# Lightning attention and a highway layer on one core: a second written-out order of all engines

## The chip, the core and the metric

The kernel runs on one core of a Trainium2 chip. The core has five engines that work side by side, each through its own queue of instructions in program order: TensorE (PE) for products, VectorE (DVE), ScalarE (ACT), GpSimd (POOL) and SyncE (SP), which here issues the transfers. They wait for each other by semaphores only. The metric is the device time of one execution in microseconds.

## The reference

Attention with a decay per head, over 4 batches, 8 heads, 768 positions of 64 elements, is followed by a highway layer over the 3072 tokens of 512 features that come out of it:

```python
for b in range(nb):
    intra = (qb @ kb.T * Dmask) @ vb                   # inside a block
    inter = (qb * lam_pow) @ kv_state                  # from all blocks before
    out[block] = intra + inter
    kv_state = lam_block * kv_state + (kb * rev_pow).T @ vb
x = out.transpose(0, 2, 1, 3).reshape(B * S, H * D)
H = maximum(x @ w_h, 0)
T = 1 / (1 + exp(-(x @ w_t + b_t)))
result = T * H + (1 - T) * x                           # = x + T * (H - x)
```

Everything is given and returned as 32-bit floats.

## The kernel before

The tokens are cut into 12 tiles (n = 0 to 11) of 256 positions, three to a batch; a tile has two rows b of 128. The order of the work is not found by a scheduler: it is written out in a string `PLAN`, and the loop at the end of the kernel emits one piece of work for each token of it. Each engine gets its pieces in the order in which they stand there, so PLAN is five queues in one. After the dots stand the tile (or group) and its parts, after `@` the engine, after `=` the numbers of the buffers or PSUM banks that the piece takes.

Loads, all on SP: `Lk.n.p`, `Lq.n.p`, `Lv.n.p` bring half (four heads, 256 KB) of a tile of k, q, v; `W.w.g` brings half (512 KB) of w_h (w = 0) or w_t (w = 1); `ST.n` stores a tile (512 KB), `ST.11.b.p` a part of the last one.

Preparing, mostly on POOL: `CK` casts k to bf16, `CQ` and `CV` cast q and v and scale them by powers of the decay (part 2 means the whole tile), `WC.w.g.i` casts a quarter of a weight. `LB` makes the powers: a product spreads the eight decay factors (the row `lam_r`) over the partitions, then come a logarithm and two exponentials. `PT` loads ACT's table for the sigmoid; `B` and `BC` turn the bias into a column.

Attention: `TK`, `TQ` transpose k and q on PE, `EK`, `EQ` copy the results out of PSUM. `SA.n` and `SB.n` compute a tile's scores together with its state products (the state stays in PSUM; `SA` needs the tile's scaled v), `KE.n.b` copies the state out, `M.n.e.u` applies the decay mask (always DVE), `I` multiplies by the state, `A.n.u` the masked scores by v, and `D.n.b` takes a finished row out as `xT`.

Highway: rows are joined into ten groups g (two rows in groups 0 to 3 and 7, four in 4 to 6, one in 8 and 9). `F.g.u.w` is a product with w_h or w_t, `H` makes max(h, 0) - x (DVE), `G` the sigmoid (ACT), `X` multiplies the two (DVE or POOL), `R` adds x and turns the result back on PE, `E` copies it out for the store.

`Z.r` issues r idle products of zeros in which nothing is computed; they fill time in which PE would wait.

Of the kernel before, what the change touches and what calls it, by code (L numbers as in the profile page):

```python
# [26 lines left out]
A.0.1=1 M.1.0.0=5 M.1.1.0=6 Z.3=0 TK.2.2=0 CK.3.2@POOL=0 KE.1.0@ACT=2 SB.1=5 EK.2.2@ACT=2 KE.1.1@ACT=3 M.1.0.1=7
WC.1.0.0@ACT A.0.0 D.0.0@ACT=0 I.1.0=2 I.1.1=4 WC.1.0.1@DVE A.1.0 A.1.1 Z.1=0 TQ.2.2=0 D.1.1@ACT=1 D.1.0@ACT D.0.1@DVE
Z.1=5 F.0.0.1=5 BC G.0.0 EQ.2.2@DVE I.2.0=3 CQ.3.2@POOL=1 WC.0.0.1@DVE F.0.0.0=6 H.0.0=0 X.0.0@DVE=0 WC.1.1.1@ACT
WC.1.1.0@ACT F.1.0.1=1 G.1.0 F.1.0.0=0 SA.2=426 H.1.0=1 CV.3.2@POOL=3 M.2.1.0=0 M.2.1.1=3 M.2.0.0=1 Lk.7.1 SB.2=5  # L30
F.1.1.1=0 F.0.1.1=2 WC.0.1.0@ACT KE.2.0@ACT=0 I.2.1=6 G.0.1 F.0.1.0=4 Lv.7.0=2 Lv.7.1 A.2.0 M.2.0.1=2 X.1.0@DVE=1
A.2.1 D.2.0@ACT=2 TK.3.2=5 F.1.1.0=1 Lq.8.0=3 CQ.4.2@POOL=0 D.2.1@DVE F.2.0.0=6 Lq.8.1 Lk.8.0=3 Lk.8.1 Lv.8.1=3 G.1.1
H.0.1=2 X.0.1@DVE H.1.1=0 EK.3.2@ACT=0 X.1.1@DVE TQ.3.2=3 EQ.3.2@ACT H.2.0=1 F.2.1.0=4 H.2.1=2 R.1=25 E.1.0@ACT=0
R.0=10 E.0.1@ACT=1 SA.3=364 KE.3.0@ACT=1 M.3.1.0=5 F.2.0.1=2 M.3.0.0=6 TQ.4.2=0 SB.3=6 M.3.1.1=4 CK.4.2@ACT=1 Lv.8.0
M.3.0.1=7 CV.4.2@POOL=0 TK.4.2=3 I.3.1=4 E.0.0@ACT A.3.0=1 EQ.4.2@ACT=1 KE.3.1@ACT=2 E.1.1@DVE EK.4.2@DVE A.3.1
D.3.1@DVE=1 F.2.1.1=6 SA.4=053 M.4.0.0=0 M.4.1.0=1 D.3.0@ACT CQ.5.2@POOL=2 F.3.0.1=1 G.2.1 X.2.1@DVE=1 F.3.0.0=4
H.3.0=0 KE.4.0@ACT=3 CK.5.2@POOL=2 Lk.9.1=4 Lk.9.0 G.2.0 Lq.9.1=4 X.2.0@DVE G.3.0 M.4.1.1=2 SB.4=0 KE.4.1@ACT=0
TK.5.2=5 EK.5.2@ACT=2 TQ.5.2=6 F.3.1.0=4 X.3.0@DVE=0 H.3.1=2 F.3.1.1=2 EQ.5.2@ACT M.4.0.1=3 CV.5.2@POOL=1 SB.5=3
# [43 lines left out]
def kernel(  # L82
# [11 lines left out]
    nc = tc.nc  # L94
    B, H, S, D = q.shape
# [9 lines left out]
    singles = ctx.enter_context(tc.tile_pool(name="singles", bufs=1))  # L105
# [3 lines left out]
    V, A, P, T = nc.vector, nc.scalar, nc.gpsimd, nc.tensor  # L109
# [279 lines left out]

    def powers():  # L390
        t = bank(("lam",), [128, H])
        T.matmul(t, lhsT=ones, rhs=lam_r, start=True, stop=True)
        A.activation(ln_bc, t, AF.Ln)
        V.tensor_tensor(p_ln, in0=ln_bc[:, None, :, None].to_broadcast([128, NST, H, J]),
                        in1=tk_f[:, :, None, :].to_broadcast([128, NST, H, J]), op=ALU.mult)
        A.activation(pow_q, p_ln, AF.Exp)
        A.activation(pow_v, p_ln, AF.Exp, scale=-1.0)
        A.dma_start(out=bt_r, in_=moe_b_t.rearrange("(j p) -> j p", p=128))

    def spin(r, idle=[0]):  # L400
        idle[0] += 1
# [57 lines left out]
```

## Time and profile before

| | us |
|---|---|
| three runs | 107.06, 107.11, 108.89; median 107.11 |
| the profiled execution | 106.9 |
| its span, first to last instruction | 105.1 |
| PE busy, of the span | 97.1 |
| DVE, ACT, POOL busy | 80.1, 70.3, 59.9 |
| mean rate of all transfers | 262 GB/s |

The span is one execution as the hardware profiler saw it, and the times of pieces below come from it. PE's busy time includes its idle products, and the ends of products are modelled, so a full PE says only that nothing keeps it waiting. In the views, a time in brackets is how long the engine was idle before an instruction, and the name after the arrow is what ended the wait; "issue" means that the profile shows nothing that it waited for.

### The profile page before, as it was taken

The page shows a single profiled execution, that of the slowest core. Times are in us where ns is not written, and L with a number is a line of the kernel's source. Part 1 is how long each engine was busy: PE and PEld are TensorE (multiplying, and loading weights), DVE is VectorE, ACT ScalarE, POOL GpSimd, SP SyncE. Part 2 cuts the span into 40 slices and gives each one's busy share as a digit, 9 for nine tenths or more (in the row PEclk, how much of TensorE's full clock was granted, in tenths as well). Part 3 has the DMA queues.
Part 4 walks back from the last instruction along what each step waited for, and adds up shares of the span by engine and source line. Part 5 has one row for each costly group of instructions (what it writes and reads, how often), then busy time and mean ns, then how long its engine had stood idle before and what let it go on. Part 6 is the DMA issues. An engine that isn't in the chain of part 4 may idle for free.

```text
span 105.1 us, 4749 instructions
## 1 busy us (share of the span) xinstructions
PE 97.1 (92%) x2087; PEld 69.1 (66%) x2087; DVE 80.1 (76%) x138; ACT 70.3 (67%) x120; POOL 59.9 (57%) x51
## 2 busy tenths in 40 slices
PE   4997999999999999999999999999899999995950
PEld 1434565778888887988465776575586567785930
DVE  4347187946979898997899799889697797995660
ACT  4228334787668998969579897366886556575860
POOL 6200886536479569859959789989496300700000
PEclk9999999999999999999999999999999999999996
DMA  1999999999999999999999999999960005994593
GB/s 40 287 316 291 290 290 329 324 334 314 291 292 292 298 288 278 293 280 295 263 305 301 296 267 279 317 315 331 363 204 14 0 6 190 377 377 171 204 359 130
DMA packets 43582, 27.57 MB, mean 262 GB/s; under 512 B 1446, under 2 KB 40618, under 8 KB 43562
## 3 DMA queue, kind: packets, MB, share of 16 engines
q1 hardware_dynamic: 43552, 27.27, 90.4%
q8 instruction: 16, 0.26, 1.1%
q14 instruction: 4, 0.03, 0.1%
q10 hardware_dynamic: 10, 0.00, 0.0%
HBM read 20.97 MB, written 6.29 MB: 259 GB/s over the span
## 4 chain that ended last, share of the span: by engine, by line
PE 84%; DMA 4%; ACT 3%; issue 2%; SPq 1%; DVE 1%; ACTq 0%; DVEq 0%
PE bt L332 21%; PE bh L332 20%; PE bs L238 7%; PE bo L306 7%; PE bktr L218 6%; PE bx L376 5%; PE bspin L404 5%; PE bqtr L218 5%; PE bo L295 5%; DMA kf<-in_k_dram 4%; PE kv L243 4%; SPq L183 1%; ACT L419 1%; ACT bt L343 1%; DVE th L346 1%
## 5 line engine op out<-in xcount | busy, mean ns | idle before, releaser
L332 PEld LDWEIGHTS <-w_b 128*128 128x128 bf16 x320 | 27.3, 98 | 12.5 <-issue 1.2
L280 DVE TENSOR_TENSOR m<-bs,tri 128x512 bf16<-128x512 f32 x48 | 30.6, 680 | 2.5 <-PE bs L238 1.9
L201 POOL TENSOR_TENSOR vs<-vf,pow_v 128x1024 bf16<-128x1024 f32 (+1 forms) x13 | 22.1, 1706 | 14.1 <-DMA vf<-in_v_dram 13.1
L332 PE MATMUL bt<-xT,w_b 128*128 128x256 bf16 (+2 forms) x160 | 24.5, 294 | 1.2 <-issue 1.1
L332 PE MATMUL bh<-xT,w_b 128*128 128x256 bf16 (+2 forms) x160 | 24.3, 294 | 0.0
L336 DVE SCALAR_TENSOR_TENSOR hm<-bh,xT 128x512 bf16<-128x512 f32 (+1 forms) x26 | 16.5, 645 | 6.5 <-PE bh L332 4.5
L201 POOL TENSOR_TENSOR qb<-qf,pow_q 128x1024 bf16<-128x1024 f32 (+1 forms) x11 | 20.1, 1827 | 2.1 <-DMA qf<-in_q_dram 2.1
L343 ACT ACTIVATE bt<-bt,bt_col 128x256 f32<-128x256 f32 (+2 forms) x34 | 15.4, 461 | 6.5 <-PE bt L332 3.8
L117 ACT ACTIVATE ss<-kv 128x512 bf16<-128x512 f32 x20 | 11.9, 596 | 4.8 <-PE kv L243 4.7
L346 DVE TENSOR_TENSOR th<-bt,hm 128x512 bf16<-128x512 f32 (+1 forms) x20 | 12.5, 632 | 1.2 <-ACT bt L343 0.2
L404 PE MATMUL bspin<-blank 128*128 128x512 bf16 x36 | 11.8, 464 | 1.4 <-DVE blank L130 1.4
L117 ACT ACTIVATE xT<-bo 128x512 bf16<-128x512 f32 x15 | 10.5, 748 | 2.8 <-PE bo L306 2.7
L238 PE MATMUL bs<-kq 64*64 64x128 bf16 x384 | 12.1, 219 | 0.0
L117 ACT ACTIVATE kq<-bktr 128x1024 bf16<-128x1024 bf16 (+1 forms) x9 | 8.4, 929 | 4.5 <-PE bktr L218 4.5
L346 POOL TENSOR_TENSOR th<-tb,hm 128x512 bf16<-128x512 f32 x6 | 6.9, 1159 | 7.6 <-DVE hm L336 7.3
L119 POOL CAST kb<-kf 128x1024 bf16<-128x1024 f32 (+1 forms) x9 | 8.5, 944 | 3.9 <-DMA kf<-in_k_dram 3.8
L238 PEld LDWEIGHTS <-kq 64*64 64x64 bf16 x384 | 9.0, 107 | 1.0 <-issue 0.2
L119 DVE CAST xT<-bo 128x512 bf16<-128x512 f32 x9 | 6.5, 732 | 3.3 <-PE bo L306 3.3
L243 PE MATMUL kv<-vs,kb 64*64 64x64 bf16 x320 | 8.7, 195 | 0.0
L117 ACT ACTIVATE o<-bx 128x512 f32<-128x512 f32 x13 | 7.4, 597 | 2.0 <-DMA out_dram<-o 1.0
L218 PE MATMUL bktr<-id,kb 128*128 128x128 bf16 x96 | 7.7, 220 | 0.8 <-ACT kb L117 0.7
L243 PEld LDWEIGHTS <-kb 64*64 64x64 bf16 x320 | 6.8, 109 | 2.6 <-issue 1.5
(55 smaller groups left out, 121.5 us busy)
## 6 DMA issues: line engine op xcount, KB each, us to landing
kf<-in_k_dram SPq DMA_DIRECT2D x24, 256.0 KB, 5.6
qf<-in_q_dram SPq DMA_DIRECT2D x24, 256.0 KB, 5.3
vf<-in_v_dram SPq DMA_DIRECT2D x24, 256.0 KB, 5.5
out_dram<-o SPq DMA_DIRECT2D x11, 512.0 KB, 4.2
w_f<-in_moe_w_t_dram SPq DMA_DIRECT2D x2, 512.0 KB, 7.4
w_f<-in_moe_w_h_dram SPq DMA_DIRECT2D x2, 512.0 KB, 7.7
out_dram<-oq SPq DMA_DIRECT2D x1, 256.0 KB, 2.2
out_dram<-oh SPq DMA_DIRECT2D x2, 128.0 KB, 1.8
```

The source lines that it names most:

```text
L117: A.activation(dst, src, AF.Copy)
L119: ENG[eng].tensor_copy(dst, src)
L201: ENG[eng].tensor_tensor(dst, in0=get(src, n)[:, heads(p)].rearrange("p h (j d) -> p h j d", j=J), in1=pw[:, n % NST, heads(p), :, None].t ...
L218: T.transpose(t[:, i, j, :], get(x + "b", n)[:, j, h:h + 2, :], id128)
L238: T.matmul(get("s", n, e, hp // 2)[half(b), hp % 2, j, :], lhsT=kq(n)[half(e), 0, hp, j, half(b)], rhs=kq(n)[half(e), 1, hp, :, half(b)], ...
L243: T.matmul(kv[half(e), hp, half(e)], lhsT=get("kb", n)[half(b), j, 2 * hp + e, :], rhs=get("vs", n)[half(b), 2 * hp + e, j, :], start=firs ...
L280: V.tensor_tensor(new(("m", n, e, u), [128, 2, J, C]), in0=get("s", n, e, u), in1=tri[:, None].to_broadcast([128, 2, J, C]), op=ALU.mult)
L332: T.matmul(t[:, r, :], lhsT=w_b[w][:, kc, m * 128:(m + 1) * 128], rhs=xT(g)[:, kc, :], start=(kc == 0), stop=(kc == KC - 1))
L336: V.scalar_tensor_tensor(new(("hm", g, u), [128, len(rows(g, u)), size(g) * C], tag=f"hm{size(g)}"), in0=get("h", g, u), scalar=0.0, in1=x ...
L343: A.activation(get("tt", g, u)[:, r, :], t[:, r, :], AF.Sigmoid, bias=bt_col[:, m:m + 1])
L346: ENG[eng].tensor_tensor(new(("th", g), [128, NP, size(g) * C], tag=f"th{size(g)}")[:, span(g, u), :], in0=get("tt", g, u), in1=get("hm", ...
L404: T.matmul(t, lhsT=blank[:, 0:128], rhs=blank, start=True, stop=True)
```

## The change

The whole of PLAN is replaced. The same pieces are there, with these differences: six `KE` move from ACT to DVE, other copies and casts change engines (three `EK` and two `D` go to ACT, two `E` to DVE, two weight casts to POOL), and 35 idle products stand in place of 36. The order on every engine, the order of the loads and the buffers are new; the order was planned with five sets of fetch delays. Beside it, the bias is brought by a transfer that ACT issues right behind that of the decay factors, not behind the exponentials; `PT` stands later; and the first three idle products and the product that spreads the factors read constants that the program sets up in any case, so that the tile `ones` goes.

The plan's opening, the place around the last tiles and the end, before and after:

```diff
-Z.4=0 LB=6 Z.8=0
-Lk.1.1=0 Lq.1.1=0 CQ.1.1@DVE=0 Lq.0.1=1 CQ.0.1@DVE=1 TQ.0.1=0 Lk.0.0=1 Lq.0.0 PT CK.0.0@ACT=0 CK.1.1@POOL=1
-Lv.0.0=0 Lk.0.1 Lv.0.1 CV.0.1@POOL=0 Lk.1.0 CK.1.0@POOL CQ.0.0@DVE Lq.1.0 CQ.1.0@POOL Lv.1.1=1 CV.1.1@POOL=1 Lv.1.0
-CV.1.0@POOL Lk.2.0=2 Lk.2.1 CK.2.2@POOL=2 Lq.2.0=2 Lq.2.1 CQ.2.2@POOL=2 W.1.0 W.0.0 Lv.2.1=2 WC.0.0.0@POOL Lv.2.0
-TQ.1.1=1 W.1.1 TK.1.1=2 CV.0.0@DVE W.0.1 Lk.3.0=3 Lk.3.1 Lq.3.1=3 Lq.3.0 Lv.3.0=3 Lv.3.1 Lq.4.1=4 Lq.4.0 TK.0.0=3
-CV.2.2@POOL=2 Lk.4.1=4 Lk.4.0 Lv.4.0=4 Lv.4.1 Lq.5.1=1 Lq.5.0 Lk.5.1=0 Lk.5.0 Lv.5.0=0 CK.0.1@ACT Lv.5.1 Z.9=4
-TK.0.1=4 Lq.6.1=0 Lk.6.0=1 TQ.0.0=5 Lk.6.1 WC.0.1.1@POOL B=6 Lq.6.0 EQ.0.1@ACT=0 EK.1.1@DVE=1 EK.0.0@DVE EK.0.1@ACT
-EQ.0.0@DVE Z.2=0 SA.0=230 KE.0.0@ACT=0 Lv.6.1=1 Lv.6.0 M.0.1.1=0 M.0.1.0=1 M.0.0.0=2 Z.5=4 TQ.1.0=4 EQ.1.0@DVE
-TK.1.0=5 SB.0=0 EQ.1.1@DVE I.0.1=3 EK.1.0@ACT M.0.0.1=3 KE.0.1@ACT=1 Z.3=2 SA.1=245 M.1.1.1=4 Lq.7.1=2 Lq.7.0 Lk.7.0=2
-A.0.1=1 M.1.0.0=5 M.1.1.0=6 Z.3=0 TK.2.2=0 CK.3.2@POOL=0 KE.1.0@ACT=2 SB.1=5 EK.2.2@ACT=2 KE.1.1@ACT=3 M.1.0.1=7
-WC.1.0.0@ACT A.0.0 D.0.0@ACT=0 I.1.0=2 I.1.1=4 WC.1.0.1@DVE A.1.0 A.1.1 Z.1=0 TQ.2.2=0 D.1.1@ACT=1 D.1.0@ACT D.0.1@DVE
-Z.1=5 F.0.0.1=5 BC G.0.0 EQ.2.2@DVE I.2.0=3 CQ.3.2@POOL=1 WC.0.0.1@DVE F.0.0.0=6 H.0.0=0 X.0.0@DVE=0 WC.1.1.1@ACT
-WC.1.1.0@ACT F.1.0.1=1 G.1.0 F.1.0.0=0 SA.2=426 H.1.0=1 CV.3.2@POOL=3 M.2.1.0=0 M.2.1.1=3 M.2.0.0=1 Lk.7.1 SB.2=5
-F.1.1.1=0 F.0.1.1=2 WC.0.1.0@ACT KE.2.0@ACT=0 I.2.1=6 G.0.1 F.0.1.0=4 Lv.7.0=2 Lv.7.1 A.2.0 M.2.0.1=2 X.1.0@DVE=1
...
-D.3.1@DVE=1 F.2.1.1=6 SA.4=053 M.4.0.0=0 M.4.1.0=1 D.3.0@ACT CQ.5.2@POOL=2 F.3.0.1=1 G.2.1 X.2.1@DVE=1 F.3.0.0=4
...
-Lk.10.0=0 Lk.11.0=1 Lk.10.1 ST.1 Lq.10.0 CV.8.2@POOL=0 CK.9.2@POOL=0 SB.8=6 SA.8=104 X.4.1@POOL TK.9.2=2 D.7.0@ACT
...
-SB.9=0 M.9.0.1=5 F.5.2.1=4 F.5.0.1=1 G.5.2 G.5.0 M.9.0.0=6 X.5.2@DVE=1 X.5.0@DVE I.8.0=2 E.5.1@ACT I.8.1=3 F.5.1.0=0
-I.9.1=5 A.9.1=4 A.8.1 KE.9.1@ACT=0 A.8.0 H.5.1=0 X.5.3@POOL A.9.0 CQ.11.2@POOL=0 CK.10.2@POOL=1 TK.10.2=6 D.8.0@DVE=0
-D.9.1@DVE CQ.10.2@POOL=2 TQ.10.2=1 Lv.11.1 TQ.11.2=0 CK.11.2@ACT=2 TK.11.2=2 D.9.0@ACT D.8.1@ACT F.6.3.1=4
-EQ.10.2@DVE=1 EK.11.2@DVE=2 CV.10.2@POOL=2 X.5.1@POOL F.6.3.0=5 EQ.11.2@DVE H.6.3=3 EK.10.2@ACT SA.10=316 G.6.3=1
-R.7=20 R.6=45 M.10.1.1=5 M.10.1.0=7 M.10.0.0=1 E.7.1@DVE=3 KE.10.0@ACT=1 SB.10=6 E.7.0@ACT CV.11.2@POOL=3 F.6.2.1=2
-G.6.2 KE.10.1@ACT=2 F.6.2.0=1 H.6.2=2 M.10.0.1=2 X.6.2@DVE=0 I.10.0=3 F.6.1.1=0 G.6.1=2 F.6.0.0=1 H.6.0=1 I.10.1=6
...
-M.11.0.1=4 F.7.1.0=3 G.7.1 I.11.1=1 X.6.0@DVE ST.4 M.11.1.0=6 A.11.1 A.11.0 X.6.3@POOL R.9=62 X.7.0@DVE=1 H.7.1=0
-D.11.0@ACT=0 X.7.1@DVE E.9.0@ACT=1 R.8=53 E.8.1@ACT=3 D.11.1@DVE=1 E.8.0@DVE R.10=04 E.10.0@DVE=0 F.8.0.1=1 E.9.1@ACT
-F.9.1.0=6 F.8.0.0=3 H.8.0=0 G.8.0 E.10.1@ACT X.8.0@DVE=0 F.8.1.1=5 F.8.1.0=2 F.9.1.1=0 F.9.0.1=4 G.8.1 H.8.1=1
-X.8.1@DVE G.9.1 F.9.0.0=3 R.11.0.2=1 ST.2 ST.8 H.9.1=2 X.9.1@DVE=1 R.11.1.1=2 H.9.0=0 G.9.0 ST.10 X.9.0@DVE ST.9
-E.11.0.2@ACT=0 ST.11.0.2 E.11.1.1@DVE=0 ST.11.1.1 R.11.1.0=5 E.11.1.0@ACT=1 ST.11.1.0
+Y.3=0 LB=6 Z.11=0
+Lv.0.1=0 CV.0.1@POOL=0 Lq.0.1=0 Lq.0.0 Lk.1.1=0 CQ.0.0@DVE=0 CK.1.1@POOL=0 TK.1.1=0 TQ.0.0=1 CQ.0.1@POOL Lk.1.0
+CK.1.0@ACT Lk.0.0=1 CK.0.0@ACT=1 Lk.0.1 Z.5=2 TK.0.0=2 Lv.0.0 Lq.1.0=1 Lv.1.1=1 CV.1.1@POOL=1 TK.1.0=3 TQ.0.1=4
+EQ.0.0@DVE=0 EQ.0.1@DVE Lq.1.1 CQ.1.1@POOL=1 W.0.1 Lv.1.0 CK.0.1@ACT TK.0.1=5 EK.0.0@ACT EK.1.0@ACT=1 EK.0.1@ACT W.0.0
+Lq.2.0=2 WC.0.1.0@POOL WC.0.0.0@POOL Lq.2.1 CQ.2.2@POOL=2 Lk.2.1=2 Lk.2.0 CK.2.2@POOL=2 Lv.2.1=2 Lv.2.0 W.1.1
+CV.2.2@POOL=2 W.1.0 WC.1.0.1@POOL WC.1.0.0@POOL Lk.3.1=3 Lq.3.0=3 Lq.3.1 CQ.3.2@POOL=0 CV.0.0@DVE Lk.3.0 Lv.3.1=3
+Z.5=1 SA.0=612 KE.0.0@ACT=0 Z.3=3 SB.0=4 CQ.1.0@DVE Lv.3.0 M.0.1.1=0 TQ.1.0=3 Lq.4.0=4 Lq.4.1 EQ.1.0@ACT Z.1=2
+TQ.1.1=5 M.0.0.0=1 M.0.1.0=2 I.0.1=2 M.0.0.1=3 WC.0.1.1@ACT A.0.1=6 CV.1.0@DVE EK.1.1@ACT KE.0.1@ACT=1 A.0.0
+D.0.1@ACT=0 EQ.1.1@ACT Z.7=1 SA.1=134 M.1.0.0=4 D.0.0@ACT KE.1.0@ACT=2 F.0.1.0=0 WC.0.0.1@ACT SB.1=2 M.1.1.0=5
+F.0.0.0=5 I.1.1=6 Lk.4.0=4 I.1.0=1 Lk.4.1 M.1.1.1=6 M.1.0.1=7 A.1.1 A.1.0 D.1.1@ACT=1 D.1.0@DVE Lv.4.1=4 B=3 Lv.4.0
+KE.1.1@DVE=3 BC TQ.2.2=4 EQ.2.2@DVE=2 H.0.1=0 H.0.0=1 Lq.5.0=0 TK.2.2=2 F.1.1.0=1 EK.2.2@ACT CK.3.2@POOL=1 F.1.0.0=6
+WC.1.1.0@DVE SA.2=342 SB.2=0 Lq.5.1 WC.1.1.1@ACT F.1.1.1=5 Lk.5.1=0 PT Lk.5.0 M.2.1.1=0 M.2.1.0=3 KE.2.0@ACT=0 I.2.1=2
+M.2.0.1=1 G.1.1 Lv.5.0=0 F.0.1.1=4 F.1.0.1=0 G.1.0 Lv.5.1 H.1.1=2 F.0.0.1=1 X.1.1@DVE=0 Lq.6.0=1 I.2.0=5 A.2.1
+M.2.0.0=2 A.2.0 G.0.1 H.1.0=2 X.1.0@DVE X.0.1@DVE=1 D.2.1@DVE=2 R.1=36 TQ.3.2=0 G.0.0 D.2.0@ACT X.0.0@DVE Lk.6.1=1
...
+D.3.1@ACT SA.4=203 M.4.1.0=0 M.4.1.1=1 F.3.0.0=1 F.3.1.0=5 Lk.7.1 CV.5.2@POOL=1 Lv.7.0=2 Lv.7.1 CK.6.2@POOL=1 G.2.0
+KE.4.0@ACT=0 SB.4=0 M.4.0.0=2 X.2.0@DVE I.4.1=3 KE.4.1@ACT=3 TK.5.2=2 M.4.0.1=3 TQ.5.2=6 EK.5.2@ACT=2 H.3.1=1
+F.3.0.1=0 A.4.0 EQ.5.2@DVE H.3.0=2 SA.5=526 M.5.1.1=4 M.5.0.0=7 CQ.6.2@POOL=0 M.5.1.0=5 A.4.1 G.3.0 D.4.0@ACT=0
+F.3.1.1=1 KE.5.0@ACT=2 SB.5=6 M.5.0.1=6 CV.6.2@POOL=2 X.3.0@DVE=1 TK.6.2=4 I.5.0=5 I.5.1=2 A.5.0 A.5.1 D.4.1@ACT G.3.1
...
+X.4.0@DVE I.7.1=3 A.7.0 A.7.1 D.7.1@ACT Lv.9.0 D.7.0@DVE Lk.11.0=1 Lq.10.1=0 Lq.10.0 CV.8.2@POOL=0 Lk.10.1 ST.1
...
+CQ.10.2@POOL=1 R.4=56 M.9.0.0=5 Lk.11.1 KE.9.0@ACT=0 SB.9=4 Lv.10.1 F.5.1.0=3 KE.9.1@DVE=3 F.5.2.1=2 Lq.11.1=1
+M.8.0.1=6 E.4.0@ACT=0 E.4.1@ACT CK.10.2@ACT=0 I.8.0=5 I.9.1=6 G.5.2 ST.3 Lv.11.1=1 Lq.11.0 M.9.0.1=4 H.5.1=3 M.9.1.0=7
+F.5.2.0=0 H.5.2=2 TQ.10.2=4 EQ.10.2@ACT=1 F.5.1.1=3 G.5.1=0 CV.10.2@POOL=2 CK.11.2@POOL=2 X.5.3@POOL=1 ST.5 X.5.2@DVE
+ST.4 I.8.1=1 TK.10.2=0 Lv.11.0 EK.10.2@DVE A.9.1=2 A.9.0 D.9.0@ACT=0 D.9.1@DVE A.8.1 A.8.0 SA.10=430 D.8.0@ACT
+I.10.0=6 F.5.0.1=2 G.5.0 D.8.1@DVE M.10.1.1=2 M.10.1.0=4 M.10.0.0=5 F.6.2.0=5 F.6.3.1=1 X.5.0@DVE KE.10.0@DVE=2
+TK.11.2=0 CQ.11.2@POOL=2 H.6.2=2 F.6.0.0=3 H.6.0=1 EK.11.2@ACT=0 TQ.11.2=4 X.5.1@POOL R.6=25 G.6.3=1 E.6.1@ACT=3
+EQ.11.2@ACT E.6.0@ACT R.7=03 E.7.0@DVE=4 E.7.1@DVE SB.10=1 CV.11.2@POOL=3 F.6.3.0=5 M.10.0.1=7 H.6.3=0 KE.10.1@ACT=0
...
+F.7.1.0=4 M.11.0.0=3 X.6.2@DVE F.7.1.1=5 G.7.1 H.7.1=0 ST.7 ST.6 ST.2 A.11.1 A.11.0 X.6.1@POOL R.9=03 D.11.1@DVE=0
+R.8=24 F.7.0.1=6 E.8.1@ACT=0 F.7.0.0=4 E.9.0@DVE=1 X.7.1@DVE=0 E.9.1@DVE ST.9 E.8.0@DVE ST.8 F.9.0.0=0 D.11.0@ACT=1
+F.9.0.1=5 H.7.0=2 F.8.0.1=1 F.8.0.0=3 F.8.1.1=2 G.7.0 G.9.0 X.7.0@DVE H.9.0=0 R.10=46 G.8.0 H.8.0=1 X.9.0@DVE=0
+X.8.0@DVE=1 F.8.1.0=0 H.8.1=2 G.8.1 E.10.1@ACT=4 F.9.1.1=3 R.11.1.0=5 E.10.0@ACT ST.10 F.9.1.0=1 G.9.1 X.8.1@DVE
+R.11.0.2=6 E.11.1.0@DVE=0 E.11.0.2@ACT=0 ST.11.1.0 ST.11.0.2 H.9.1=0 X.9.1@DVE R.11.1.1=0 E.11.1.1@DVE=1 ST.11.1.1
```

The rest of the diff:

```diff
     bt_r = singles.tile([KC, 128], F32)
+    A.dma_start(out=bt_r, in_=moe_b_t.rearrange("(j p) -> j p", p=128))
...
-    ones = singles.tile([1, 128], F32)
-    V.memset(ones, 1.0)
...
     def powers():
         t = bank(("lam",), [128, H])
-        T.matmul(t, lhsT=ones, rhs=lam_r, start=True, stop=True)
+        T.matmul(t, lhsT=nc.const_aps.tensor(1.0, [1, 128], F32), rhs=lam_r, start=True, stop=True)
...
-        A.dma_start(out=bt_r, in_=moe_b_t.rearrange("(j p) -> j p", p=128))
+
+    def spin_ones(r):
+        t = bank(("spin", 0), [128, 512])
+        for _ in range(r):
+            T.matmul(t, lhsT=nc.const_aps.tensor(1.0, [128, 128], BF16), rhs=nc.const_aps.tensor(1.0, [128, 512], BF16),
+                     start=True, stop=True)
...
+        "LB": lambda a, e: powers(), "Y": lambda a, e: spin_ones(*a), "PT": lambda a, e: A.preload_act_table(AF.Sigmoid),
```

## The prediction

> **What bounds the kernel now.** I read the page first, then the time by windows, then the timeline at each place where TensorE (PE) idles, then the landings of the loads. The page and the windows (columns: window, PE, PEld, DVE, ACT, POOL busy, clock, DMA share, GB/s):
>
> ```profile
> PE 97.1 (92%) x2087; PEld 69.1 (66%) x2087; DVE 80.1 (76%) x138; ACT 70.3 (67%) x120; POOL 59.9 (57%) x51
> PE 84%; DMA 4%; ACT 3%; issue 2%; SPq 1%; DVE 1%; ACTq 0%; DVEq 0%
> ...
> 70.00:75.00 5.00, 4.80 (x112) 3.03 (x105) 4.81 (x9) 3.85 (x8) 4.87 (x4) 1.00 1.08 343
> 75.00:80.00 5.00, 4.73 (x114) 3.50 (x117) 3.39 (x6) 3.59 (x5) 3.02 (x2) 1.00 0.61 190
> 80.00:85.00 5.00, 5.00 (x146) 3.28 (x139) 4.29 (x8) 2.43 (x5) 1.90 (x1) 1.00 0.02 3
> 95.00:98.00 3.00, 1.89 (x36) 1.77 (x33) 1.21 (x3) 1.81 (x5) 0.00 (x0) 1.00 0.51 187
> ```
>
> PE carries 84% of the chain. From 22 to 95 us it is full except around 75; the waits at 95.5 and after 99.8 lie behind that. The loads come at some 290 GB/s without a pause until about 80 us. So there are three bounds in turn: loads before 22 us, PE to 95 us, a chain of short steps at the end. The body's PE work is the same in both orders, so the change can gain only before SA.2, in PE's stalls and at the end, and can lose anywhere.
>
> PE has two stalls that no other engine ends (start, duration, in brackets the idle time before and what ended it):
>
> ```profile
> 74.51 0.30 PE L306 MATMUL bo<-m,vs 64*64 64x128 bf16 x6
> 75.27 1.02 PE L306 MATMUL bo<-m,vs 64*64 64x128 bf16 x58 [0.46 <-issue]
> ...
> 94.97 0.51 PE L332 MATMUL bt<-xT,w_b 128*128 128x128 bf16 x6
> 96.59 0.27 PE L332 MATMUL bt<-xT,w_b 128*128 128x128 bf16 x2 [1.11 <-issue]
> ```
>
> Both break off inside one product, A.9.1 and F.8.0.1. Counted in PE's instruction list they stand at places 3008 and 4032, exactly four times 256 apart, and the page has 16 transfers of 16 KB (256 instructions of 64 B) on q8, kind "instruction". In the packet records the last before each stall start at 72.70 and 94.19 and take 1.02 and 0.92; PE goes on 1.5 us after each ends. These are waits for code: 0.46 + 1.11 = **1.57 us**.
>
> **Part 1, the code waits.** With boundaries every 256 instructions, the 15 fetches in the records that can be placed start 0.26 to 3.68 us after PE crosses a boundary (median 1.4), take about 1.1, and count 1.5 later. PE must need some 4.0 us to the next boundary, 5.2 at a start of 2.6, to see nothing. I summed the work between boundaries with rows of before (F 0.87 or 0.45, eight transposes 0.45, SA 0.61, R 0.47, A 0.21). Before has stretches of 3.0 us (R.1 to SB.3) and 2.1 us (A.11.1 to F.8.0.1: three R in a row, 96 matmuls of 28 ns each). After has none under 4.2 (SB.4 to SB.5); the next are 4.6 and 4.7, the rest 4.8 to 6.3. Real stretches run 4% above these sums. The long wait at the end should go. What remains is open: 0 if starts stay near 1.4; about 1.5 if the 15 starts fell at random on the new stretches. The last quarter has little data in flight (80 to 85: 3 GB/s), and there the starts were 0.26 to 1.21, so I take 0.8. Gain **0.8**, ends 0 and 1.57.
>
> [...]
>
> **Part 2, the opening.** Loads are issued on SP in order; the first lands at 3.83, each 256 KB one 0.9 later, a W 1.5 to 2.2. Lv.2.0 is 20th on SP in both orders with two W ahead (it landed at 23.23), so the scale that feeds SA.2 cannot move:
>
> ```profile
> 23.36 1.90 POOL L201 TENSOR_TENSOR vs<-vf,pow_v 128x1024 bf16<-128x1024 f32 x1 [1.24 <-DMA vf<-in_v_dram]
> ...
> 25.75 0.22 PE L243 MATMUL kv<-vs,kb 64*64 64x64 bf16 x2
> ```
>
> It ends at 25.27; before starts SA.2 at 25.75, after four F and I.2.0. After has four F ahead too, without I.2.0. Can it be there in time? W.0.1, now 12th, lands near 15.3 (13.25 for the 11th, and two loads' time). ACT then casts it (WC.0.1.1), and behind that cast, in ACT's order, stand EK.1.1, KE.0.1, D.0.1, EQ.1.1: 5 steps at a pitch of 0.5 to 0.6, so SA.1 near 18.1 (before 16.6). Then D.0.0, first F 18.8 (before 21.95), SB.1, F, I, masks (four at 0.6 after SA.1), A.1 to 22.0, D.1 0.75, two F: 24.9. PE waits for CV.2.2 until 25.3 and is 0.45 - 0.22 = 0.2 ahead.
>
> It is lost at once. The sigmoid's table load (1.28 us on ACT) leaves a place where the loads covered it (7.22, before CK.0.0) for one behind WC.1.1.1, whose W.1.1 lands at 24.69: 24.7 + 0.6 + 1.28 + KE.2.0's 0.6 = 27.3, and I.2.1 would be due at 27.0. Then R.1 needs X.1.0: F.1.0.1 done 29.5, G.1.0 0.93, X.1.0 0.69: 31.2 against 31.0. R.1 ends at 31.7; the same work in before ends at 31.6 (34.38 less two F and 16 transposes). Net **+0.1**, ends -0.5 and +0.6.
>
> At no cost: idle products are 35 instead of 36 and stand where PE waits. Three now read constants set at 0.4 us and start some 0.6 earlier than 1.38, but the factors' product waits for its 3.2 anyway. [...] The bias transfer costs ACT's queue 0.25 us ahead of its first table load (then until about 2.9; its next step is at 3.83): covered by 0.9. Leaving its old place, it takes no wait off: CK.0.0 needed its load and the table. B and BC move behind A.1.0, before the first sigmoid. The memset of 0.17 was idle DVE's.
>
> **Part 3, the body.** Six KE go from ACT (0.60) to DVE (about 0.68), three EK and two D the other way: DVE +2, ACT -2, POOL +1 (two more casts) over 60 us, against 25, 35 and 45 idle. At nothing while order holds. By the same count of loads and POOL's steps, SA.3 to SA.9 have their v scale 0 to 2 us before PE comes: SA.4 at 39.7 against a scale that ended at 39.53, and before is as tight (39.55).
>
> The one place where cover goes is SA.10:
>
> ```profile
> 76.39 1.90 POOL L201 TENSOR_TENSOR vs<-vf,pow_v 128x1024 bf16<-128x1024 f32 x1 [1.52 <-DMA vf<-in_v_dram]
> ...
> 79.84 0.22 PE L243 MATMUL kv<-vs,kb 64*64 64x64 bf16 x2
> ```
>
> Before has 1.55 us between the scale (ends 78.29) and SA.10 (79.84). After holds back F.5.0.1, the two F.6.3 and tile 11's transposes (2.6 + 0.9), so that PE, without the stall of 0.46, reaches SA.10 about 4 us earlier, at 75.7. Lv.10.1, on which CV.10.2 now waits, lands between 73.5 (its place in the queue by count) and 74.7; CV.10.2 takes 1.9. PE waits 0 to 0.9; I take **+0.3**. Behind SA.10 stand PE's whole queue, and on POOL CK.11.2, X.5.3, CQ.11.2, X.5.1 (5.3 us, the last due for R.6 at 81.4): they slip with it, so it is paid once. Lv.11.0, last load, stands behind four stores instead of three: lands about 82, CV.11.2 done at 84, SA.11 at 85.
>
> **Part 4, the end.**
>
> ```profile
> 100.97 0.42 DVE L346 TENSOR_TENSOR th<-bt,hm 128x256 bf16<-128x256 f32 x1
> 101.31 0.41 DVE L119 COPY oh<-bx 128x256 f32<-128x256 f32 x1
> 101.45 0.23 PE L355 MATMUL bx<-id,th 128*128 128x128 bf16 x1 [0.46 <-DVE th L346]
> ```
>
> After R.10 (95.04) before needs 10.06 us to 105.1: 4.49 of PE work, 1.11 for code, so 4.46 idle. In after, from the end of R.8 DVE has the long list: E.9.0, X.7.1, E.9.1, E.8.0, H.7.0, X.7.0 (0.6 each, 0.8 where X follows its own H), then ten steps of group 8 and 9 (0.33, dependent 0.45), paced from F.8.1.0 on by PE. Followed step by step X.9.1 ends 7.3 us after R.8, R.11.1.1 and E.11.1.1 at 8.15; issue, landing and close take 2.9 as in before (102.21 to 105.1): 11.05. PE's work in it is 6.74, so 4.3 idle: **-0.15**, ends -0.6 and +0.6.
>
> **Sum.** -0.8 + 0.1 + 0.3 - 0.15 = -0.55. The profiled execution took 106.9 (span 105.1 and 1.8 around it), so 106.35; the median of the runs is 107.11, 0.2 above that execution, so the forecast is **106.6**.
>
> **Rivals.** (a) All code waits gone and v in time: -1.57 + 0.1 - 0.15: **105.5**. For it: no stretch under 4.2. Against: two of 15 starts over 3 us. (b) Slower: the v scale of tile 10. If Lv.10.1 lands at 75.5, where it landed in before, CV.10.2 ends at 77.4 and SA.10 waits 1.7, not 0.3: **108.0**. It decides from a landing of 74.8 on. Against: by count one load fewer stands ahead of it, if SP is never held. (c) Code waits move instead of going: SB.4 to SB.5 (4.4 real) with the start of 3.23 seen at 69.5 needs 5.8, a wait of 1.4; two like it and 106.6 becomes **108.6**. (d) Only the order is another, and waits of PE that I do not see eat the gain: **107.1**.
>
> **Chances.** Forecast 0.36 (105.9 to 107.2), (a) 0.22, (b) 0.18, (c) 0.12, (d) 0.12, part of each beyond 109. A measurement of this kernel tells about 2% from no change: below 105.0 (a, with a better end) 0.13; above 109.3 (b and c together, or an unseen wait) 0.17. Range 104.9 to 108.9.
>
> **What would show it.** Right: no PE stall of 1 us marked "issue" near the end, SA.2 within 0.3 of 25.3, KE.2.0 behind a table load near 25.4, a short wait at SA.10. Wrong: SA.2 after 26, SA.10 waiting over 1 us for POOL, "issue" over 1.5 us in sum, or DVE idle between R.8 and the last store.

## The result, and the profile after

The changed kernel took 106.72 us (median of 22 runs, 105.62 to 108.56), beside 108.09 for the kernel before in the same rounds (22 runs, 106.94 to 112.95). The ratio is **0.9933, with a 95% interval of 0.9905 to 0.9961**: faster, by some 0.7 us. In some executions of either kernel the time is over 1.5% above that kernel's fastest; the ratios leave these out, so the medians lie further apart than the ratio says, and the first profile of after (107.84 us) was one of them. Three more sets of runs of the same kernel gave 0.9917 [0.9872, 0.9962], 0.9930 [0.9885, 0.9975] and 0.9962 [0.9920, 1.0004].

The profile shown here is therefore that of a_same, the changed kernel run once more (span 103.6). The page, then the windows (columns as before):

```profile
PE 96.2 (93%) x2075; PEld 68.9 (67%) x2086; DVE 80.9 (78%) x139; ACT 68.5 (66%) x116; POOL 61.4 (59%) x53
...
PE 76%; SPq 7%; DMA 6%; ACT 4%; DVE 2%; issue 1%; DVEq 0%
```

```profile
70.00:75.00 5.00, 4.95 (x47) 3.08 (x50) 4.45 (x8) 4.04 (x6) 2.37 (x2) 1.00 1.12 349
75.00:80.00 5.00, 4.95 (x130) 3.38 (x131) 4.95 (x9) 2.22 (x5) 5.00 (x5) 1.00 0.92 331
80.00:85.00 5.00, 4.95 (x145) 3.32 (x148) 3.99 (x7) 4.00 (x6) 1.62 (x2) 1.00 0.14 48
95.00:98.00 3.00, 3.00 (x77) 2.85 (x75) 2.48 (x7) 2.70 (x8) 0.00 (x0) 1.00 0.90 330
```

PE is full where before had its two holes: 4.95 in place of 4.80 and 4.73, and 3.00 of 3 us in place of 1.89. "issue" goes from 2% of the chain to 1%. The timeline of a_same at the places that the prediction named (start, duration, in brackets the idle time before and its releaser):

```profile
24.74 0.22 PE L242 MATMUL kv<-vs,kb 64*64 64x64 bf16 x2
...
25.31 1.28 ACT L423 ACT_TABLE_LOAD   x1
26.61 0.60 ACT L117 ACTIVATE ss<-kv 128x512 bf16<-128x512 f32 x1
...
27.26 0.40 PE L294 MATMUL bo<-kq,ss 128*128 128x128 bf16 x4 [0.65 <-ACT ss L117]
...
72.64 1.90 POOL L200 TENSOR_TENSOR vs<-vf,pow_v 128x1024 bf16<-128x1024 f32 x1 [2.73 <-DMA vf<-in_v_dram]
...
75.86 0.19 PE L242 MATMUL kv<-vs,kb 64*64 64x64 bf16 x2
...
99.87 0.23 PE L354 MATMUL bx<-id,th 128*128 128x128 bf16 x1 [0.62 <-DVE th L345]
```

SA.2 starts at 24.74; the table load holds KE.2.0 and with it I.2.1 for 0.65; SA.10 comes at 75.86, 4 us earlier than in before, and here its scale is done 1.3 us ahead; the last wait is the known one for the last th.

### The profile page after: what moved, and what is told of

The parts are those of the page before. It is cut to its first block, busy times and chain, and to the rows that moved or that the text cites. A ratio compares the mean times of both kernels' runs of the same rounds, so it can differ in the third digit from the quotient of the medians.

```text
span 106.1 us, 4755 instructions
## 1 busy us (share of the span) xinstructions
PE 96.6 (91%) x2086; PEld 68.7 (65%) x2086; DVE 81.5 (77%) x139; ACT 68.7 (65%) x116; POOL 61.5 (58%) x53
## 4 chain that ended last, share of the span: by engine, by line
PE 32%; SPq 24%; DMA 19%; DVE 9%; POOL 7%; issue 5%; POOLq 0%; DVEq 0%
SPq L182 22%; DMA vf<-in_v_dram 12%; PE bh L331 10%; PE bt L331 9%; DMA qf<-in_q_dram 8%; PE bx L375 4%; DVE m L279 4%; POOL qb L200 3%; DVE th L345 3%; POOL vs L200 3%; PE bs L237 2%; PE bktr L217 2%; DVE hm L335 2%; PE bo L305 2%; SPq L186 2%
## 5 line engine op out<-in xcount | busy, mean ns | idle before, releaser
L200 POOL TENSOR_TENSOR vs<-vf,pow_v 128x1024 bf16<-128x1024 f32 (+1 forms) x12 | 21.1, 1761 | 12.5 <-DMA vf<-in_v_dram 12.5
L200 POOL TENSOR_TENSOR qb<-qf,pow_q 128x1024 bf16<-128x1024 f32 (+1 forms) x12 | 21.1, 1761 | 4.4 <-DMA qf<-in_q_dram 4.4
L117 ACT ACTIVATE xT<-bo 128x512 bf16<-128x512 f32 x17 | 12.1, 747 | 4.7 <-PE bo L305 4.6
L117 ACT ACTIVATE kq<-bktr 128x1024 bf16<-128x1024 bf16 (+1 forms) x12 | 10.3, 879 | 3.9 <-PE bktr L217 3.8
L117 ACT ACTIVATE ss<-kv 128x512 bf16<-128x512 f32 x14 | 8.4, 598 | 3.4 <-PE kv L242 3.2
L117 ACT ACTIVATE o<-bx 128x512 f32<-128x512 f32 x12 | 6.9, 595 | 3.7 <-DMA out_dram<-o 2.1
L217 PE MATMUL bqtr<-id,qb 128*128 128x128 bf16 x96 | 7.7, 220 | 1.5 <-POOL qb L200 1.5
L408 PE MATMUL bspin<-blank 128*128 128x512 bf16 x32 | 8.9, 416 | 0.0
L117 ACT ACTIVATE kq<-bqtr 128x1024 bf16<-128x1024 bf16 (+1 forms) x7 | 6.3, 900 | 3.6 <-PE bqtr L217 3.6
```

The source lines that it names most:

```text
L117: A.activation(dst, src, AF.Copy)
L200: ENG[eng].tensor_tensor(dst, in0=get(src, n)[:, heads(p)].rearrange("p h (j d) -> p h j d", j=J), in1=pw[:, n % NST, heads(p), :, None].t ...
L217: T.transpose(t[:, i, j, :], get(x + "b", n)[:, j, h:h + 2, :], id128)
L408: T.matmul(t, lhsT=blank[:, 0:128], rhs=blank, start=True, stop=True)
```

## The experiments

Two means are used throughout. In the packet records each fetch of 16 KB of PE's code can be timed (16 in before, 0.92 to 1.77 us each); a crossing, below, is the moment at which PE starts on the next 256 instructions. And `K.r` is an idle product like `Z.r`, but of 128 columns, so that four K last about as long as one Z (in before's trace, from 9 us on, products of 128 columns follow each other every 56 ns, idle ones of 512 every 216): replacing Z by K moves all later boundaries of 256 instructions earlier in the work and leaves the work alone. Two theories stand against each other in the expectations: theory one, that waits for code cost PE their length and are what the change gains, and its rival, that the new order itself gains.

**After again, and moved boundaries.** a_same is after unchanged. The others:

```diff
 b_p96, of before:  Z.9 -> K.34,  Z.5 -> K.19,  Z.3 (ahead of SA.1) -> K.12     (+96 instructions)
 b_p64, of before:  Z.9 -> K.34,  Z.3 (ahead of SA.1) -> K.10                   (+64)
 a_p112, of after:  both Z.5 -> K.19,  Z.3 -> K.11,  Z.7 -> K.27                (+112)
```

> The changed kernel once more, for a second profile and as the companion of the three beside it. Both theories (code waits; order of the engines) expect what was measured: 0.993 of before, within 0.004. In the profile: no PE wait of 0.4 us or more marked issue after 30 us; SA.10 waiting for the v scale of tile 10, CV.10.2, by 0.3 to 1.

> Before, with 29 more pairs... in the place of 17 idle products of 512 columns in the opening (Z.9, Z.5, the first Z.3) stand 65 of 128 columns, which fill the same time (0.0555 us each) and move every later boundary of 256 instructions on PE by 96 instructions. Nothing else differs. The two shortest stretches of PE work between boundaries, 2.3 and 3.2 us, become 4.2 and 3.0. Theory of code waits: the wait at F.8.0.1 (1.11 us) and that at A.9.1 (0.46) go, some 0.3 may come at the stretch of 3.0: 1.0 to 1.5 us less, 0.986 to 0.991 of before. Theory that the order is what gains: 1.000.

> Before, with 44 small idle products in the place of 12 large ones (Z.9 and the first Z.3): every later boundary on PE moves by 64 instructions, which makes the stretches worse: 2.6, 2.6 and 3.3 us. Theory of code waits: over the 15 starts of fetches seen in before, these stretches cost 1.2 us more than those of before on average: 1.005 to 1.015. Theory that the order is what gains: 1.000.

> The changed kernel, with 76 small idle products in the place of 20 large ones in the opening (both Z.5, Z.3, Z.7): boundaries on PE move by 112 instructions, and its shortest stretches become 3.5 and 3.5 us (as it was: 4.5 and 4.9). Theory of code waits: 1.0 to 1.2 us of waiting comes back, 1.002 to 1.006 of before instead of 0.993. Theory that the order is what gains: 0.993 still.

Measured: a_same 0.9917; b_p96 1.0095 [1.0021, 1.0170]; b_p64 0.9966 [0.9917, 1.0014]; a_p112 1.0036 [0.9975, 1.0098]. The order alone doesn't set the time, since equal orders differ. But two forecasts missed. b_p64 was to be slower and was not: its profile has one wait for code after SA.2, of 0.53. And b_p96 was to be the fast one and was the slowest. a_p112 came out at the number expected, but that doesn't show the reason: its profile has three waits for code, 0.70 and 0.35 in the opening, where loads set the pace (256 KB in some 0.9 us in before), and one of 0.47 behind it, and its times are spread more widely than those of any other kernel here (106.8 to 113.8). PE's waits in b_p96 (waited for: us in total, times, longest) show that the two old waits are gone, and that there are three new ones, the longest in the opening, at 19 us:

```profile
PE bo L306 <- issue: 1.6, 1, 1.6
...
PE bx L376 <- issue: 1.1, 1, 1.1
PE kv L243 <- issue: 0.8, 1, 0.8
```

Each breaks off at a boundary again, as the second does inside a row of R.2 (timeline of b_p96):

```profile
50.90 0.19 PE L376 MATMUL bx<-id,th 64*128 64x64 bf16 x1
52.16 0.20 PE L376 MATMUL bx<-id,th 64*128 64x64 bf16 x1 [1.07 <-issue]
```

The fetch for it ran from 49.56 to 50.77. The next one started only at 56.32, 4.2 us after PE had crossed the boundary at 52.16, ended at 57.40, and PE waited for it until 58.91. I had put starts of 0.3 to 3.7 us in the order in which before's profile had them; they don't stay in place.

**A smaller shift in both orders, and two parts of the change alone.** The same edit in both orders, PT back in after, and the small edits alone in before:

```diff
 b_p32, of before
-Z.5=4 TQ.1.0=4
+K.21=4 TQ.1.0=4
 a_p32, of after
-Z.5=2 TK.0.0=2
+K.21=2 TK.0.0=2
 a_pt, of after
-CK.1.0@ACT Lk.0.0=1 ...   Lk.5.1=0 PT Lk.5.0
+PT CK.1.0@ACT Lk.0.0=1 ...   Lk.5.1=0 Lk.5.0
 b_code, of before: the bias transfer, the constants (Y.4 for Z.4) and the end of `ones`
```

> The order of before, with 21 idle products of 128 columns in place of 5 of 512 ahead of TQ.1.0 (as long, 16 products and 32 instructions more), so that every later crossing into a new stretch of 256 instructions falls 32 instructions earlier in the work. From the crossing times and fetch starts of six profiles, the waits for code should shrink from 1.57 us to about 0.2 us. Theory one (the whole gain of the change is the two waits for code that are gone; the new order itself is worth nothing): span near 103.7 us, ratio to before 0.984 to 0.991, as good as the change itself, with no wait over 0.3 us without a named releaser after 20 us. Rival (the new order gives the gain): ratio 0.998 to 1.002.

> The order of after with the same edit: 21 idle products of 128 columns in place of 5 of 512 ahead of TK.0.0, 32 instructions more. From the same model the waits for code should grow from nothing to about 2.2 us (near 18.9, 74 and 79 us). Theory one (waits for code are the whole difference): span near 105.8 us, ratio to before 1.003 to 1.015. Rival (the new order gives the gain): ratio 0.990 to 0.994, like after.

> After with the table load PT put back to the opening, ahead of CK.1.0 on ScalarE, where before has it, in place of its new place ahead of KE.2.0. If the 0.65 us for which I.2.1 waits on KE.2.0 near 27 us in after's profile is on the path to the end: I.2.1 without that wait, span down 0.4 to 0.7, ratio to before 0.985 to 0.988 (after 0.992). Rival: the time is taken back by a later wait (loads or POOL near SA.10, or a wait for code, whose crossings then come earlier while fetches start no earlier): ratio 0.990 to 0.994.

> Before's order with the three small edits alone: bias transfer issued behind the factors' row, first four idle products from constants, the row of ones gone; as many TensorE instructions as before. Theory one: nothing past the first 10 us moves, ratio 0.997 to 1.003, and both waits for code stay. Rival (the opening edits carry a part of the gain): KB and SA.0 0.3 to 0.5 us earlier and so the end, ratio 0.994 to 0.997.

Measured: b_p32 1.0007 [0.9962, 1.0051], a_p32 1.0008 [0.9964, 1.0052], a_pt 0.9953 [0.9914, 0.9992], b_code 1.0018 [0.9978, 1.0057]. b_code is as theory one said: the small edits bring nothing, and its profile has the waits for code again (0.19 at 75.3 and 1.08 at 95.7). b_p32 missed: in its profile the waits are 0.34, 0.18 and 0.36, not 0.2 in sum, and it isn't faster. a_p32 came out slower than after, though not by as much as expected, and its profile has one wait of 0.63 near 18 and one of 0.29 near 77, not 2.2. Early PT gained nothing: I.2.1's wait is gone, but the other profiles of after don't have it either, and TK.5.2 waits 0.82 for POOL instead. By then theory one could neither be upheld nor dropped.

**What holds the fetches up.** In before's windows the DMA engines are full until 77 us (share 1.07 from 70 on) and nearly idle from 79 to 88 (0.02), and there fetches start 0.3 to 0.7 us after the crossing. So stores were moved on SP's queue, with PE's list untouched:

```diff
 b_st, of before: ST.1, ST.3, ST.0, ST.5, ST.4 behind Lv.11.1
 a_st, of after:  ST.1, ST.3, ST.5, ST.4 behind Lv.11.0
```

> Before with stores moved on SyncE's queue alone: ST.1, ST.3, ST.0, ST.5 and ST.4 stand behind the last load Lv.11.1, where the DMA engines are idle from 79 to 88 us; TensorE's list and all other lists stay. Theory one (fetches of code stand behind data in the DMA engines, and the two waits for code are on the path to the end): the fetch after the crossing at 93.0 finds the engines idle and starts 0.2 to 0.6 us after it (1.21 in before), so that the wait of 1.11 us near 95.5 shrinks to 0 to 0.4; the wait of 0.46 near 75 becomes 0 to 0.5; span 104.0 to 104.5, ratio 0.988 to 0.994, without any of the new order. Rival (these waits are not what sets the end, or the fetch start doesn't depend on the stores): ratio 0.998 to 1.002. A second rival: the stores at 76 to 83 now hold up the fetches after 75.3 and 80.2 by over 2.3 us, with new waits near 80 or 86, ratio 0.998 to 1.005.

> After with the same kind of move: ST.1, ST.3, ST.5 and ST.4 behind the last load Lv.11.0. Each store holds the engines about 1.27 us, so Lv.10.1 lands 1.3 us earlier, Lv.11.0 4 to 5 us earlier. Theory one (in most runs of after little is left to gain here: no wait for code, and SA.10's wait for Lv.10.1 between 0 and 0.9 us): ratio to before 0.986 to 0.993, at or up to 0.5 us below a_again. Rival (the supply of SA.10 costs after nothing on average): as a_again within 0.2 us.

> After unchanged, beside the two others on the same chip: ratio 0.990 to 0.995, no wait for code over 0.3 us past 20 us.

Measured: b_st **1.0506** [1.0447, 1.0565], a_st **1.0648** [1.0581, 1.0715], a_again 0.9962. A store holds the engines for 1.38 to 1.40 us where one follows another in before, not for 1.27. I had overlooked what a store gives free: ScalarE's copy E waits until its output buffer has been stored, and PE behind it (timeline of b_st):

```profile
77.27 0.60 ACT L117 ACTIVATE o<-bx 128x512 f32<-128x512 f32 x1 [5.73 <-DMA out_dram<-o]
...
77.92 1.01 PE L295 MATMUL bo<-kq,ss 128*128 128x128 bf16 x8 [4.34 <-ACT o L117]
```

So these stores may be moved earlier, not later. The late part of b_st still answers: from SA.11 to the last wait in R.11.1.0 it takes 13.84 us, against 15.12 in before.

**Stores moved earlier.** Before's late wait ends on a fetch that starts 1.21 us behind the crossing at 93.0. At that time the DMA engines are busy with stores (share 1.01 from 88 to 95, at 371 GB/s): ST.6, ST.7, ST.5, ST.4 and ST.2 follow each other from 88 to 95. Two ways of having them out of the way:

```diff
 b_st54, of before: ST.5 ST.4 directly behind Lv.11.1
 b_st754, of before
-ST.6 A.10.1 ... ST.7 ST.5 F.7.0.0=3 ... ST.4 M.11.1.0=6
+ST.7 ST.5 ST.4 ST.6 A.10.1 ... F.7.0.0=3 ... M.11.1.0=6
 a_lv, of after: Lk.11.1 and Lv.10.1 exchanged
```

> Before with two stores alone moved on SyncE's queue: ST.5 and ST.4, whose rows are ready at 74.3 us, stand behind the last load Lv.11.1 instead of behind ST.7, so that they move at 80 to 84 us, where the DMA engines are idle, and not at 91 to 94. No store is later than in before, so no output buffer comes free later; TensorE's list is the same. Theory one (the fetch of code after the crossing at 93.0 stands behind these stores, and the wait that follows from it is on the path to the end): that fetch starts 0.2 to 0.7 us after the crossing (1.21 in before), the wait of 1.11 us near 95.5 shrinks to 0 to 0.5 us; span down by 0.6 to 1.1 us, ratio 0.990 to 0.995, as good as the whole change. Rival one (the wait isn't tied to the stores): wait of 1.0 to 1.2 still there, ratio 0.998 to 1.002. Rival two (wait gone, and the end where it was, because ScalarE, VectorE or the last stores set it): wait under 0.5 and ratio 0.998 to 1.002.

> Before with the order of four stores on SyncE's queue changed and nothing else: ST.7, ST.5, ST.4, ST.6 in place of ST.6, ST.7, ST.5, ST.4. ST.7's rows are ready at 83.2 us and ST.6's at 87.0, so three stores move at 83.5 to 87.5, in the idle time of the DMA engines, and all are through by 92 us, ahead of the crossing at 93.0. Other than in b_st54 no store stands near the crossings at 75.3 and 80.2. Theory one (the wait of 1.11 us for code near 95.5 is tied to the stores and costs its length): the fetch after the crossing at 93.0 starts 0.2 to 0.7 us behind it, the wait is 0 to 0.4 us, SA.11 to R.11.1.0 takes 13.8 to 14.2 us (15.1 in before), ratio 0.988 to 0.994. Rival one (the wait is not tied to them): 15.1 us, ratio 0.998 to 1.002. Rival two (the wait goes and the end doesn't move, since ScalarE, VectorE or the last stores set it): wait gone, ratio 0.998 to 1.002.

> After with the loads Lv.10.1 and Lk.11.1 exchanged on SyncE's queue, so that Lv.10.1, which SA.10 waits for in one of three profiles of after by 0.64 us (0.34 us behind TK.10.2 in another), lands 0.75 us earlier; Lk.11.1 lands 0.75 us later and is used 3 us later. Theory one (the supply of SA.10 costs after 0.2 to 0.4 us on average): ratio to before 0.988 to 0.991, no wait at SA.10 over 0.2 us. Rival (such waits are made up by others, or rare): ratio 0.991 to 0.996 as after itself.

Measured: b_st54 0.9969 [0.9924, 1.0013]; **b_st754 0.9884** [0.9817, 0.9952]; a_lv 0.9918 [0.9878, 0.9959]. In b_st54 the late wait is gone, but the fetch after 75.83 started 3.84 us behind it and another wait took its place (timeline of b_st54):

```profile
82.06 0.35 PE L238 MATMUL bs<-kq 64*64 64x128 bf16 x10 [1.15 <-issue]
```

In b_st754 it is gone and nothing took its place. The windows around the late crossing, of before and then of b_st754 (the last figure is GB/s), show the stores gone from there:

```profile
93.00:94.00 1.00, 1.00 (x68) 0.91 (x68) 0.90 (x2) 0.43 (x1) 0.00 (x0) 1.00 1.02 375
...
93.00:94.00 1.00, 1.00 (x53) 0.81 (x52) 0.90 (x3) 0.27 (x2) 0.00 (x0) 1.00 0.01 2
```

Where before waited 1.11 us inside F.8.0.1, PE goes from R.10 through the products (timeline of b_st754; no bracket means no wait):

```profile
95.15 0.19 PE L376 MATMUL bx<-id,th 64*128 64x64 bf16 x2
95.27 0.62 PE L332 MATMUL bt<-xT,w_b 128*128 128x128 bf16 x8
95.73 1.06 PE L332 MATMUL bh<-xT,w_b 128*128 128x128 bf16 x16
```

The fetches follow the stores in both directions: after the crossing at 86.25, which now has them in flight, the fetch starts 3.01 us later (0.26 in before; the stretch of 7 us hides it), and by the crossing at 93.28 the next has begun. From SA.11 to the last wait in R.11.1.0 it takes 13.85. Four stores put in another order on one queue bring about as much as the whole plan. a_lv has no long wait at SA.10 but is level with after.

**Again, and both waits out.** b_st754_2 is b_st754, a_again2 is after, b_st_k11 and b_st_k11_2 are b_st754 with one more edit:

```diff
-Z.3=0 TK.2.2=0
+K.11=0 TK.2.2=0
```

> The same kernel as b_st754 (before with the stores in the order ST.7, ST.5, ST.4, ST.6), once more and beside after itself. Theory one (the late wait for code costs its 1.1 us, and the rest of the new order brings nothing on balance): ratio 0.986 to 0.993, at or below after's. Rival (the first result was luck of three runs; after's order has a gain of its own): 0.994 to 1.000, above after's.

> After unchanged on the same chip as b_st754_2 and b_st_k11: ratio 0.990 to 0.996.

> b_st754 with 11 idle products of 128 columns in place of 3 of 512 ahead of TK.2.2 (8 products, 16 instructions more), so that the crossings after 20 us fall 16 instructions earlier in the work. By the crossing times and fetch starts of the profiles the wait of 0.46 us near 75 should go or shrink, and one of 0.1 us come near 37. Theory one (every wait for code on TensorE costs its length): 0.2 to 0.4 us below b_st754_2, ratio 0.983 to 0.990. Rival (a wait in mid-run is made up later, by loads, or moves to another crossing): equal to b_st754_2 within 0.2 us.

> The same kernel as b_st_k11, once more. Theory one (before's order without its two waits for code is worth 1.5 us and beats after): ratio 0.983 to 0.990. Rival (the first result was luck; it equals after): 0.991 to 0.997.

Measured: b_st754_2 0.9879 [0.9795, 0.9964], a_again2 0.9930, b_st_k11 **0.9856** [0.9783, 0.9930], b_st_k11_2 0.9891 [0.9807, 0.9976]. These intervals are wide, and the medians over all executions show less of the gain of b_st754: 106.73 and 107.04, beside 107.15 and 107.50 for before. All of PE's waits listed for b_st_k11_2:

```profile
PE bspin L404 <- DVE blank L130: 1.4, 1, 1.4
PE bktr L218 <- ACT kb L117: 1.3, 1, 1.3
PE bt L332 <- issue: 0.5, 2, 0.3
PE bx L355 <- DVE th L346: 0.5, 1, 0.5
```

Of the two short "issue" waits one (0.32) lies before SA.2, the other is 0.16 long; none of before's waits for code is left. That is the version to keep from these runs, but it isn't shown to beat after: the intervals overlap, and the medians over all executions don't part them (106.24 and 106.45; after 106.31 to 106.72).

**The sum over the profiles.** From the start of SA.2 to the end of the last copy E, with PE's waits for code in that stretch ("issue" gaps of over 0.15 us in which no weight load runs either):

| order of before | us | for code | rest |
|---|---|---|---|
| before | 76.45 | 1.57 | 74.88 |
| b_code | 76.41 | 1.27 | 75.14 |
| b_p96 | 76.68 | 1.88 | 74.80 |
| b_p64 | 75.13 | 0.53 | 74.60 |
| b_p32 | 75.77 | 0.88 | 74.89 |
| b_st54 | 76.14 | 1.32 | 74.82 |
| b_st754 | 75.23 | 0.45 | 74.78 |
| b_st754_2 | 74.44 | 0 | 74.44 |
| b_st_k11 | 74.50 | 0 | 74.50 |
| b_st_k11_2 | 74.87 | 0 | 74.87 |

Ten profiles with before's order (b_st, with its stall of another kind, left out): the stretch varies by 2.2 us, less its waits for code by 0.7. On this order every such wait costs its whole length at the end. The same stretch in four profiles of after (after, a_same, a_again, a_again2): 77.43, 75.92, 75.87, 76.85, with waits for code of 0, 0, 0.34 and 0.

## Why the prediction was right or wrong

The forecast was 0.55 us down from its execution; measured were about 0.7. That 106.72 lies beside the forecast of 106.6 says little, since 106.6 was counted from 107.11 for before, which stood at 108.09 beside the result. The sum was near because two errors offset each other.

**The step that failed is Part 3's "At nothing while order holds".** Behind SA.2 the new order loses 1.7 us; Part 2 had some 0.7 of it and SA.10's 0.3 was forecast, and most of what is left was put at nothing. The other error is one of size: Part 1 put the gain from waits for code at 0.8, and it was 1.3.

**Part 1, the code waits: right in kind, too small.** 0.8 was taken between 0 and 1.57. Before's order has 1.57 and 1.27 in two profiles (before, b_code), after 0, 0, 0.34 and 0 in four: the gain is **1.3**. The summing of stretches did see that after's order has long ones where before has 3.0 and 2.1. What failed is the step behind it, that only the late fetches start soon because little data is in flight. Starts vary from run to run: the fetch behind the crossing inside SA.7 (near 58.6) started 0.03 us after it in a_same and 2.02 in the first profile of after. In after nearly all stretches were long enough for that. Most single crossings cost nothing here (two of before's 15 placed fetches were waited for, by 0.46 and 1.11), but the sum counts: up to 1.9 us per execution after SA.2 (b_p96). Rival (c), code waits that move, did not occur in after, but it is what happened to my own b_p96 and b_st54.

**Part 2, the opening: right in time, lost in another way.** SA.2 was put at 25.3. Over the six profiles with after's order that the ratios count it stands at 24.74 to 25.80, mean 25.33; with before's order at 25.75 to 26.73 in seven, mean 26.18 (some of both with idle products exchanged). So it gains 0.85, 0.22 of it because I.2.0 now stands behind it; measured from the one early execution of before (25.75), I saw only 0.45 of this. By the end of R.1 most of it is gone, as forecast. From SA.2 to there it takes 6.62 us in seven of nine profiles with after's order, against 8.62 in every one with before's; less some 2.7 for the two F and 16 transposes that before does ahead of it, 0.7 is lost. But the loss at I.2.1 behind the table load, 0.65 in a_same, is in no other profile of after; the others lose their part in R.1, waiting for X.1.0 in pieces of 0.3 and less (last line of the first view of Part 3). Two sums of this part are off by 0.1: the steps to KE.2.0 make 27.2, and before's R.1 less the work ahead of it 31.7. And the factors' product didn't wait for its 3.2: it ran at 2.21 in the first profile of after. An earlier start gave nothing: in b_code SA.0 comes 1 us earlier than in before (11.85 for 12.82) and SA.2 no earlier (25.96).

**Part 3, the body: right at SA.10 on average, too rosy behind late loads.** SA.10 was given 0.3 (0 to 0.9). It waits 0.64, 0, 0 and 0.63 in the four profiles. In a_again2 the scale came late (waits of PE, and timeline):

```profile
PE kv L242 <- POOL vs L200: 0.6, 1, 0.6
PE bx L354 <- DVE th L345: 0.6, 1, 0.6
PE bx L375 <- DVE th L345: 0.2, 1, 0.2
```

```profile
75.62 1.90 POOL L200 TENSOR_TENSOR vs<-vf,pow_v 128x1024 bf16<-128x1024 f32 x1 [4.31 <-DMA vf<-in_v_dram]
```

Rival (b) with 1.7 did not come. But the order did not hold against late loads. This scale, CV.10.2, starts 50.1 to 50.7 us behind SA.2 in three profiles (after, a_again2, a_pt), and there the stretch to the last E takes 76.9 to 77.4; it starts 47.0 to 48.3 behind in five (a_same, a_again, a_lv, a_p112, a_p32), and there it takes 75.4 to 75.9 less waits for code. With before's order a start 50.6 and 50.8 behind SA.2 (before, b_st754) goes with 74.9 and 74.8. SA.10 follows SA.2 by 51 to 53 us in the profiles of after and by 54 in before, so it seems that before's order has slack for late loads and after's has not. No run here held the loads back on purpose, so this is a reading of profiles and not shown. The named waits are small: 0.38 at TQ.9.2 and 0.21 near 72.7 in the first profile of after, 0.82 at TK.5.2 in a_pt.

**Part 4, the end: 0 instead of -0.15.** From the end of R.8 (92.42 in a_same) to the end of the span it takes 11.2, not 11.05; the last wait for th is 0.62 in place of 0.46.

**Together.** Less waits for code, the stretch from SA.2 takes 76.4 on average in after (four profiles) against 74.8 in before's order (ten): 1.7 lost, of which I.2.0 is 0.2. In a_same nearly all of it has a name: 75.92 - 74.77 = 1.15, of which I.2.1 has 0.65, I.2.0 0.22 and the last th 0.16. In the other profiles somewhat over half has one; the rest is spread over gaps under 0.15 us, and its cause stays open. -1.3 for code, -0.85 to SA.2 and +1.7 make -0.5, and the runs say -0.7. So the re-plan's gain is the waits for code and an earlier SA.2, and most of it is given back in the body: the order itself isn't faster.

The 2% that the prediction took as the limit of what a measurement tells was too coarse: 22 runs gave an interval of 0.6% in width.

## What to carry to other kernels

Here an engine that was full and stopped for "issue" inside one product (0.46 and 1.11 us in before) was waiting for its code. To find out, count its instructions in 256s, find the fetch in the packet records, and look at what data was in flight then. The cheap remedy was on another queue: bring stores forward, out of the time in which a short stretch of code is crossed (0.9884 in b_st754), and never back past the copy that needs the buffer (1.0506 in b_st, where that copy waited 5.73 us). A new order of all engines also moves every boundary, so compare orders with the waits for code taken off before crediting the order. And when work is brought forward, ask whether its loads come forward too (a question that these profiles raise, not one that a run here settled).

## What the runs showed of the hardware

Over twenty profiles, after 20 us: of 44 crossings with the DMA engines idle (busy under a fifth of the microsecond around it) the fetch started at most 1.03 us behind, median 0.60; of some 215 with them full, median 1.55 and up to 4.16. In some 260 cases PE never entered a new stretch earlier than some 1.3 us after the end of its fetch. The order of fetch and data in the engines' queues isn't in the records, so that a fetch stands behind data is read from these lags and from b_st754, not seen directly. Equally unexpected was how far one execution is from the next at equal code: SA.2 varied by 1 us among the executions that the ratios count, which hid effects of 0.5 us from any single profile.
